# Relu, squares and low part of two blocks as one operation each, and three weight steps at later places

## The chip, the cores and the metric

The program runs on one core of a Trainium2 chip. The metric is the device time of one execution in microseconds (us). An engine works through its own queue in order: TensorE (PE, with its weight loads as PEld), VectorE (DVE), ScalarE (ACT), GpSimd (POOL) and the DMA queues (SP). A wait of one engine for another is a semaphore.

## The reference, cut to what matters

Chunked attention, then a dense MLP with a squared relu, then a top-1 mixture of eight experts, all in float32:

```python
x = attention(q, k, v, mem_k, mem_v)          # 3072 tokens, 512 wide; chunks of 32, context 16 left, 8 right
h = x @ w_in                                  # 512 -> 2048
r = np.maximum(h, 0.0)
y = (r * r) @ w_out                           # 2048 -> 512
# top-1 of 8 experts (512 -> 1024 -> 512), scaled by two gates
out[mask] = gate_w * eom * (np.maximum(y[mask] @ w1[e], 0.0) @ w2[e])
```

The change touches the dense MLP, `r * r` above all.

## The kernel before

Tokens are taken in 12 blocks of 256. A number is held as a high part that TensorE multiplies in one pass (fp32r) and a low part, the rest, also in fp32r; a product is three matmuls: high by high, high by low, low by high.

For one block `b` and one feature column group `f` of 128 (f = 0 to 15) the dense MLP is: mm1 (`ph`, 12 matmuls), relu (`r`, scaled), the square (`g`, in float32), the square again rounded to fp32r (`gh`), the low part `gl = g - gh`, and mm2 (6 matmuls into `py`, which sums over all f). In a group of two blocks most f are worked for both at once: `mm1_both` (L381) is 12 matmuls of 512 columns for the two blocks, and the two relus and mm2 follow one block at a time. For the first steps (`at[b, f] < 32`, which is blocks 0 and 1) `g` is made on ScalarE (L429), afterwards on VectorE (L431).

`seq` lists the steps: step n is one (block, f). Step n of a pair of blocks with f worked together is `mm1_both` for both, then the relu of the first block; step n + 1 is the relu of the second (L1121 to L1126). After the relu come the things planned for that step (`todo`), in the order of `turn`; at the end of a step mm2 of step n - 2 is issued. For blocks 0 and 1, f = 2 starts at step 4, and f at step 2f. The order of the queues is that of this loop: nothing is rearranged afterwards.

While blocks 0 and 1 run, the weights are converted. They arrive as 64-bit numbers in 16 tiles i0, o0, i1, o1, ..., i7, o7 of 1024 columns, two f each. One tile takes: exponent on ScalarE (`split_w_exp`, L327, "ACTIVATE ws<-raw"), a shift on VectorE (L332), two "or" steps on VectorE (L339, L343), the cast to the high part on ScalarE (`split_w_hi`, L352) and the low part on VectorE (`split_w_lo`, L357). `bits` says at which step a tile's "or" steps stand; its cast and low part stand one step later, its exponent at the end of the step of the tile before, its shift one step after that. The tile in conversion (`ws`) has two buffers, so an exponent waits for the low part of the tile two before.

Beside this runs the attention of blocks 2 and later (`plan_duo`): scores, exp, normalising, transposing the probabilities (`transpose_a`: matmuls L234, copy to `e` on ScalarE, L244), the products with v (L259).

Matmuls of the experts' pairs (`Pair`) and of its single slots come after the dense MLP; pairs use the same `gh` and `gl` pool.

Of the kernel before, what the change touches and what calls it, by code (L numbers as in the profile page):

```python
# [8 lines left out]
F32 = mybir.dt.float32  # L9
F32R = mybir.dt.float32r  # L10
# [3 lines left out]
ACTF = mybir.ActivationFunctionType  # L14
ALU = mybir.AluOpType
AX = mybir.AxisListType

P = 128
NT = 3072
D = 512  # L20
# [3 lines left out]
BLK = 256  # L24
# [22 lines left out]
WSCALE = 2.0 ** -8  # L47
# [9 lines left out]
def chunk_attention_relu2_moe_top1_kernel(ctx: ExitStack, tc, qk, vv, qt, kv, w_in, w_out, wg, wexp, consts, out):  # L57
    nc = tc.nc
# [7 lines left out]
    gp = ctx.enter_context(tc.tile_pool(name="gp", bufs=2))  # L66
# [38 lines left out]
    class Duo:  # L105
        def __init__(self, b):
            self.b = b
            self.units = (2 * b, 2 * b + 1)
            self.first, self.q, self.k, self.v = {}, {}, {}, {}
            self.ps, self.mx, self.r = {}, {}, {}  # L110
            self.e = self.at = self.x = None
            self.turned = b * TPB >= EARLY
# [209 lines left out]
    def split_w_exp(kind, g, halves=None):  # L322
        t = raw[kind, g]
        if (kind, g) not in converted:
            converted[kind, g] = tp.tile([P, 1024], F32, tag="ws", name=f"ws_{kind}{g}", bufs=2)
        for s in slices(halves):
            nc.scalar.activation(converted[kind, g][:, s], t[:, s, 1].bitcast(F32), ACTF.Abs, scale=2.0 ** -111)  # L327

    def split_w_shift(kind, g, halves=None):
        for s in slices(halves):  # L330
            li = converted[kind, g][:, s].bitcast(I32)
            nc.vector.tensor_scalar(li, li, 3, None, op0=ALU.logical_shift_left)  # L332
# [14 lines left out]
    def split_w_hi(kind, g, halves=None):  # L347
        if (kind, g) not in wh:
            w = wpool.tile([P, 2, 1024], F32R, tag=f"{kind}{g}", name=f"w{kind}{g}")
            wh[kind, g], wl[kind, g] = w[:, 0], w[:, 1]  # L350
        for s in slices(halves):
            nc.scalar.copy(wh[kind, g][:, s], converted[kind, g][:, s])  # L352
# [6 lines left out]
    def slices(halves):  # L359
        return [slice(0, 1024)] if halves is None else [slice(512 * c, 512 * c + 512) for c in halves]  # L360

    def w_in_part(w, f, k):
        return w["i", f // 2].rearrange("p (g k c) -> p g k c", g=2, k=KC)[:, f % 2, k, :]
# [2 lines left out]
        return w["o", f // 2].rearrange("p (g c) -> p g c", g=2)[:, f % 2, :]  # L366


    class Block:
        def __init__(self, b):  # L370
            self.b = b
# [9 lines left out]
        def mm1_both(self, f):  # L381
            b = self.b
            two = sorted((i % 3, i) for i in (b, b + 1))
            s = slice(two[0][0], two[1][0] + 1, two[1][0] - two[0][0])
            ph = ps_h.tile([P, D], F32, tag="h", name=f"ph{b}_{f}")
            n = 0
            for k in range(KC):
                for w, x in ((wh, xhi), (wl, xhi), (wh, xlo)):
                    nc.tensor.matmul(  # L389
                        ph.rearrange("p (s c) -> p s c", s=2),  # L390
                        lhsT=w_in_part(w, f, k),
                        rhs=x[:, s, k, :],
                        start=(n == 0),
                        stop=(n == 11),
                    )
                    n += 1
            for i, (_, of) in enumerate(two):
                blocks[of].ph = ph[:, BLK * i : BLK * i + BLK]

        def mm1(self, f):  # L400
            self.mm1_products(f)
            self.relu(f)
# [10 lines left out]
                    n += 1  # L413

        def relu(self, f):
            self.relu_r(f)
            self.relu_g(f)

        def relu_r(self, f):
            self.r = gp.tile([P, BLK], F32, tag="r", name=f"r{self.b}_{f}")  # L420
            nc.scalar.activation(self.r, self.ph, ACTF.Relu, scale=WSCALE)  # L421

        def relu_g(self, f):
            b = self.b
            early = at[b, f] < 32
            r = self.r
            g = gp.tile([P, BLK], F32, tag="g", name=f"g{b}_{f}")
            if early:
                nc.scalar.activation(g, r, ACTF.Square)  # L429
            else:  # L430
                nc.vector.tensor_tensor(g, r, r, op=ALU.mult)  # L431
            gh = gp.tile([P, BLK], F32R, tag="gh", name=f"gh{b}_{f}", bufs=3)
            nc.scalar.activation(gh, r, ACTF.Square)  # L433
            gl = gp.tile([P, BLK], F32R, tag="gl", name=f"gl{b}_{f}", bufs=3)
            nc.vector.tensor_tensor(gl, g, gh.bitcast(F32), op=ALU.subtract)  # L435
            self.g[f] = gh, gl

        def mm2(self, f):
            b = self.b
# [275 lines left out]
    class Pair(Entry):  # L715
# [13 lines left out]
        def mm1(self, f):  # L729
            p = self.entry  # L730
            ph = ps_h.tile([P, D], F32, tag="h", name=f"ph{p}p{f}")[:, :BLK]
            n = 0
            for k in range(KC):
                for part, z in ((0, self.zh), (1, self.zh), (0, self.zl)):
                    nc.tensor.matmul(
                        ph,
                        lhsT=self.w[k][:, part, f * P : f * P + P],
                        rhs=z[:, k, :],
                        start=(n == 0),
                        stop=(n == 11),  # L740
                    )
                    n += 1
            gh = gp.tile([P, BLK], F32R, tag="gh", name=f"gh{p}p{f}", bufs=3)
            nc.scalar.activation(gh, ph, ACTF.Relu)
            gl = gp.tile([P, BLK], F32R, tag="gl", name=f"gl{p}p{f}", bufs=3)
            nc.vector.scalar_tensor_tensor(gl, ph, 0.0, gh.bitcast(F32), op0=ALU.max, op1=ALU.subtract)
            self.g[f] = gh, gl

# [94 lines left out]
    tiles = [(kind, g) for g in range(8) for kind in "io"]  # L843
    duos = {b: Duo(b) for b in range(NB)}
    blocks = {b: Block(b) for b in range(NB)}


    seq, both = [], set()
    for g in range(GROUPED):
        two = (2 * g, 2 * g + 1)  # L850
# [3 lines left out]
    seq += [(NB + p, f) for p in range(NP) for f in range(F2B)]  # L854
    at = {bf: n for n, bf in enumerate(seq)}
    todo, ahead = {}, {}
    turn = {split_w_hi: 0, split_w_shift: 0, split_w_lo: 1, split_w_or: 3, split_w_exp: 4}

    def plan(n, fn, *args):
        todo.setdefault(n, []).append((fn, args))  # L860

    def plan_duo(b, s, m, t, v, last=None):
        d = duos[b]
        plan(s, d.scores)
        plan(m, d.norm)
        plan(t, d.transpose_a)
        plan(v, d.av)
        if last is None:
            plan(v, d.transpose_x_copy)
        else:  # L870
            ahead[last] = d.transpose_x_copy
        if b + 1 < NB:
            plan(s + 1, duos[b + 1].load_q, 0)
            plan(s + 1, duos[b + 1].load_q, 1)
        if 2 < b < NB - 1:
            plan(v + 1, duos[b + 1].load_kv, 1)
        if b < NB - 2:
            plan(v + 2, duos[b + 2].load_kv, 0)

    def plan_gate(b, y, l, c, r):  # L880
        bl = blocks[b]
        plan(y, bl.gate_transpose)
        plan(l, bl.gate_logits)
        plan(c, bl.gate_choose)
        plan(r, bl.gate_rank)

    bits = dict(zip(range(3, 16), (2, 4, 6, 8, 10, 12, 14, 15, 17, 18, 20, 21, 26)))
    for m, n in bits.items():
        if m > 4:
            plan(bits[m - 1], split_w_exp, *tiles[m])  # L890
            plan(bits[m - 1] + 1, split_w_shift, *tiles[m])
        if m > 3:
            plan(n, split_w_or, *tiles[m])
            plan(n + 1, split_w_hi, *tiles[m])
            plan(n + 1, split_w_lo, *tiles[m])
        if m > 6:
            plan(bits[m - 3] + 1, load_w, *tiles[m])
    plan(16, duos[2].load_q, 0)
# [6 lines left out]
    plan(23, lambda: prepare())  # L905
    n = at[2, 0]
    plan_duo(2, n - 7, n - 7, n - 4, n - 3)
    plan_duo(3, n + 1, n + 2, n + 5, n + 6)
    plan_gate(0, n + 7, n + 9, n + 15, n + 18)
    plan_duo(4, n + 11, n + 13, n + 15, n + 17)  # L910
# [2 lines left out]
    for g in range(2, GROUPED - 1):  # L913
        n = at[2 * g, 0]
# [4 lines left out]
    n = at[NB - 2, 0]  # L919
    plan_gate(NB - 4, n + 3, n + 4, n + 6, n + 9)  # L920
    plan_gate(NB - 3, n + 6, n + 8, n + 10, n + 12)
    n = at[NB, 0]
# [21 lines left out]
    for p in range(NP):  # L944
        n = at[NB + p, 0]
# [24 lines left out]
    n = at[NB, 0]  # L970
# [18 lines left out]
    with tc.manual_schedule():  # L989
# [4 lines left out]
        a, b = (0,), (1,)  # L994
# [123 lines left out]
        for n, (b, f) in enumerate(seq):  # L1118
            if n < 4:
                continue  # L1120
            if n in both:  # L1121
                blocks[b].mm1_both(f)
            if n in ahead:
                ahead[n]()
            if n in both or n - 1 in both:
                blocks[b].relu(f)  # L1126
            else:
                blocks[b].mm1(f)
            for fn, args in sorted(todo.get(n, []), key=lambda h: turn.get(h[0], 2)):
                fn(*args)  # L1130
            if n > 4:
                pb, pf = seq[n - 2]
                blocks[pb].mm2(pf)
# [148 lines left out]
```

## Time and profile before

| | before |
|---|---|
| median of 3 runs | 961.41 us (961.21 to 964.74) |
| profiled execution | 961.27 us, span 959.4 us |
| TensorE busy | 944.5 us (98%) |
| VectorE, ScalarE, GpSimd busy | 600.1, 453.0, 95.1 us |
| TensorE's granted clock | 0.999 |
| DMA | 125.51 MB, mean 131 GB/s |

Busy times are sums over the span; the idle part of TensorE has to be looked up by stretch, since the stages differ. Matmuls are pipelined, and a stall shows most exactly as idle time of the weight loads. In the rows below a line of a timeline is: start, duration, engine, source line, operation, output and inputs by their names in the program, shapes, count, and in brackets the idle time before and what ended it.

### The profile page before, as it was taken

The numbers are of one execution on the slowest core, as the hardware profiler recorded it, in microseconds if no ns is written. First come the engines' busy times: TensorE is split into PE (matmuls) and PEld (weight loads), VectorE is DVE, ScalarE is ACT, GpSimd is POOL, SyncE is SP. The second block draws the span as 40 slices with busy tenths as digits, with TensorE's granted clock in tenths as the row PEclk, the third lists the DMA queues.
The fourth block names the chain that finished last, engine by engine and source line by source line (L and its number), as shares of the span: only waits on it lengthen the run. The fifth ranks groups of instructions, "written<-read, shape, count | busy, mean of one in ns | idle before, by whom it ended". The sixth has DMA issues, their size and how long they took to land. (4 is left out here: it accounts for less than half of the span.)

```text
span 959.4 us, 19441 instructions
## 1 busy us (share of the span) xinstructions
PE 944.5 (98%) x7862; PEld 791.2 (82%) x7862; DVE 600.1 (63%) x1125; ACT 453.0 (47%) x816; POOL 95.1 (10%) x93
## 2 busy tenths in 40 slices
PE   8999999999999999999999999999999999999996
PEld 5787798888888888888888888889999999888885
DVE  6999663554445444534553454658776666799995
ACT  4687533333333233322322333545444555688885
POOL 0000000000000000000000011012222211212221
PEclk9999999999999999999999999999999999999999
DMA  9466512214020212021100106360886656443631
GB/s 358 174 219 235 170 68 99 77 24 119 24 77 24 85 58 77 24 76 59 48 1 1 45 1 247 126 241 25 333 316 237 235 206 245 187 175 132 219 124 42
DMA packets 30991, 125.51 MB, mean 131 GB/s; under 512 B 8559, under 2 KB 9071, under 8 KB 21554
## 3 DMA queue, kind: packets, MB, share of 16 engines
q1 hardware_dynamic: 25650, 110.30, 32.0%
q0 software_dynamic: 5248, 13.92, 4.0%
q8 instruction: 64, 1.05, 0.5%
q14 instruction: 29, 0.24, 0.1%
HBM read 138.65 MB, written 13.61 MB: 159 GB/s over the span
## 5 line engine op out<-in xcount | busy, mean ns | idle before, releaser
L389 PE MATMUL ph<-xhi,wi 128*128 128x512 f32 x688 | 212.7, 390 | 0.3 <-DVE wi L357 0.3
L421 ACT ACTIVATE r<-ph 128x256 f32<-128x256 f32 x192 | 72.2, 376 | 233.2 <-PE ph L389 199.1
L431 DVE TENSOR_TENSOR g<-r 128x256 f32<-128x256 f32 x160 | 67.6, 423 | 183.1 <-ACT r L421 183.0
L446 PE MATMUL py<-wo,gh 128*128 128x512 f32 x384 | 156.1, 407 | 0.8 <-ACT gh L433 0.8
L389 PEld LDWEIGHTS ph<-xhi,wi 128*128 128x128 f32 x688 | 129.1, 188 | 28.4 <-DVE wi L357 1.2
L447 PE MATMUL py<-wo,gh 128*128 128x512 f32 x384 | 150.1, 391 | 0.0
L448 PE MATMUL py<-wo,gl 128*128 128x512 f32 x384 | 150.0, 391 | 0.0
L389 PE MATMUL ph<-xlo,wi 128*128 128x512 f32 x344 | 133.9, 389 | 0.0
L686 DVE TENSOR_TENSOR x<-raw,x 128x1024 fp32r<-128x1024 f32 x88 | 103.2, 1223 | 7.0 <-ACT x L685 5.4
L435 DVE TENSOR_TENSOR gl<-g,gh 128x256 fp32r<-128x256 f32 x192 | 81.6, 425 | 29.1 <-ACT gh L433 7.3
L686 DVE TENSOR_TENSOR p<-raw,p 128x1024 fp32r<-128x1024 f32 x64 | 78.2, 1222 | 22.1 <-ACT p L685 21.0
L685 ACT CAST x<-raw 128x1024 fp32r<-128x1024 f32 x88 | 87.4, 1056 | 0.0
L446 PEld LDWEIGHTS py<-wo,gh 128*128 128x128 f32 x384 | 72.1, 188 | 17.4 <-issue 2.0
L448 PEld LDWEIGHTS py<-wo,gl 128*128 128x128 f32 x384 | 72.1, 188 | 16.1 <-DVE gl L435 0.6
L433 ACT ACTIVATE gh<-r 128x256 fp32r<-128x256 f32 x192 | 80.1, 417 | 10.6 <-PE py L447 2.3
L447 PEld LDWEIGHTS py<-wo,gh 128*128 128x128 f32 x384 | 72.3, 188 | 12.4
L543 POOL DMA_INDIRECT listd<-ent,idx x24 | 24.7, 1030 | 551.6 <-DVE idx L541 339.0
L389 PEld LDWEIGHTS ph<-xlo,wi 128*128 128x128 f32 x344 | 64.6, 188 | 13.5
L685 ACT CAST p<-raw 128x1024 fp32r<-128x1024 f32 x64 | 66.6, 1041 | 0.6 <-DMA raw<-in_wexp 0.6
L835 PE MATMUL po<-x,ht 128*128 128x512 f32 x264 | 65.5, 397 | 0.7 <-DVE ht L825 0.7
L835 PEld LDWEIGHTS po<-x,ht 128*128 128x128 f32 x264 | 48.1, 188 | 10.3 <-DVE ht L825 1.1
L705 POOL DMA_INDIRECT out<-o,slots x27 | 35.2, 1304 | 210.4 <-ACT o L701 91.4
(229 smaller groups left out, 1453.1 us busy)
## 6 DMA issues: line engine op xcount, KB each, us to landing
raw<-in_wexp SPq DMA_DIRECT2D x82, 1024.0 KB
kv<-in_kv SPq DMA_DIRECT2D x19, 880.0 KB
raw_o<-in_w_out SPq DMA_DIRECT2D x8, 1024.0 KB
raw_i<-in_w_in SPq DMA_DIRECT2D x7, 1024.0 KB
ydram<-y SPq DMA_DIRECT2D x24, 256.0 KB
q<-in_qt SPq DMA_DIRECT2D x20, 256.0 KB
qk<-in_qk SPq DMA_DIRECT2D x4, 624.0 KB
v<-in_vv SPq DMA_DIRECT2D x2, 1024.0 KB
```

What stands on the lines that cost most here:

```text
L389: nc.tensor.matmul(ph.rearrange("p (s c) -> p s c", s=2), lhsT=w_in_part(w, f, k), rhs=x[:, s, k, :], start=(n == 0), stop=(n == 11),)
L421: nc.scalar.activation(self.r, self.ph, ACTF.Relu, scale=WSCALE)
L431: nc.vector.tensor_tensor(g, r, r, op=ALU.mult)
L433: nc.scalar.activation(gh, r, ACTF.Square)
L435: nc.vector.tensor_tensor(gl, g, gh.bitcast(F32), op=ALU.subtract)
L446: nc.tensor.matmul(self.y[t], lhsT=gh[:, s], rhs=w_out_part(wh, f), start=(f == 0), stop=False)
L447: nc.tensor.matmul(self.y[t], lhsT=gh[:, s], rhs=w_out_part(wl, f), start=False, stop=False)
L448: nc.tensor.matmul(self.y[t], lhsT=gl[:, s], rhs=w_out_part(wh, f), start=False, stop=(f == NF - 1))
L685: nc.scalar.copy(w[:, 0], t)
L686: nc.vector.tensor_tensor(w[:, 1], t, w[:, 0].bitcast(F32), op=ALU.subtract)
L705: nc.gpsimd.indirect_dma_start(out=out, out_offset=bass.IndirectOffsetOnAxis(ap=slots[:, c, 0:1].bitcast(U32), axis=0), in_=self.y[t], in_ ...
L835: nc.tensor.matmul(self.po, lhsT=self.ht[:, part, f, :], rhs=w[:, wp, j * D : j * D + D], start=(f == 0 and part == 0 and wp == 0), stop=( ...
```

## The change

Relu, the rounded square, the square and the low part of two blocks are one operation of 512 columns each (`middle`, `relu_both`), all issued at the first of the two steps. The square is written over `r`, which has one buffer of 512 columns; `gh` and `gl` have two of 512 in place of three of 256. Where a block is worked alone, and in the expert pairs, two f share such a buffer by halves. The exponent of tiles 11 and 13 (o5, o6) goes to the step after, ahead of the shift (`split_w_late`), and the cast and low part of tile 15 (o7) go from step 27 to steps 28 and 29.

```diff
+    def room(b, f, n):
+        if n == D or f % 2 == 0:
+            rooms["now"] = [
+                gp.tile([P, D], dt, tag=tag, name=f"{tag}{b}_{f}", bufs=bufs)
+                for tag, dt, bufs in (("r", F32, 1), ("gh", F32R, 2), ("gl", F32R, 2))
+            ]
+        start = 0 if n == D else BLK * (f % 2)
+        return [x[:, start : start + n] for x in rooms["now"]]
+
+    def middle(ph, b, f):
+        r, hi, lo = room(b, f, ph.shape[1])
+        nc.scalar.activation(r, ph, ACTF.Relu, scale=WSCALE)
+        nc.scalar.activation(hi, r, ACTF.Square)
+        if at[b, f] < 32:
+            nc.scalar.activation(r, r, ACTF.Square)
+        else:
+            nc.vector.tensor_tensor(r, r, r, op=ALU.mult)
+        nc.vector.tensor_tensor(lo, r, hi.bitcast(F32), op=ALU.subtract)
+        return hi, lo
...
-            for i, (_, of) in enumerate(two):
-                blocks[of].ph = ph[:, BLK * i : BLK * i + BLK]
+            self.both = ph, [of for _, of in two]
+
+        def relu_both(self, f):
+            ph, two = self.both
+            parts = middle(ph, self.b, f)
+            for i, of in enumerate(two):
+                blocks[of].g[f] = tuple(x[:, BLK * i : BLK * i + BLK] for x in parts)
...
         def relu(self, f):
...
+            self.g[f] = middle(self.ph, self.b, f)
...
-            gh = gp.tile([P, BLK], F32R, tag="gh", name=f"gh{p}p{f}", bufs=3)
+            _, gh, gl = room(f"p{p}_", f, BLK)
...
+    def split_w_late(kind, g):
+        split_w_exp(kind, g)
+        split_w_shift(kind, g)
...
         if m > 4:
-            plan(bits[m - 1], split_w_exp, *tiles[m])
-            plan(bits[m - 1] + 1, split_w_shift, *tiles[m])
+            if m in (11, 13):
+                plan(bits[m - 1] + 1, split_w_late, *tiles[m])
+            else:
+                plan(bits[m - 1], split_w_exp, *tiles[m])
+                plan(bits[m - 1] + 1, split_w_shift, *tiles[m])
...
-            plan(n + 1, split_w_hi, *tiles[m])
-            plan(n + 1, split_w_lo, *tiles[m])
+            if m < 15:
+                plan(n + 1, split_w_hi, *tiles[m])
+                plan(n + 1, split_w_lo, *tiles[m])
...
+    plan(n - 4, lambda: split_w_hi(*tiles[15]))
+    plan(n - 3, split_w_lo, *tiles[15])
...
-            if n in both or n - 1 in both:
-                blocks[b].relu(f)
-            else:
+            if n in both:
+                blocks[b].relu_both(f)
+            elif n - 1 not in both:
                 blocks[b].mm1(f)
```

On ScalarE from f = 2 on, before (in a name the first number is f, the last a counter; `wi` and `wo` are casts of a weight tile, `ws` exponents):

```order
L421 ACTIVATE r_2_690<-ph_2_677 128x256
L429 ACTIVATE g_2_692<-r_2_690 128x256
L433 ACTIVATE gh_2_694<-r_2_690 128x256
L327 ACTIVATE ws_o_700<-raw_o_612 128x1024
L421 ACTIVATE r_2_702<-ph_2_677 128x256
L429 ACTIVATE g_2_704<-r_2_702 128x256
L433 ACTIVATE gh_2_706<-r_2_702 128x256
L352 CAST wi_710<-ws_i_669 128x1024
L421 ACTIVATE r_3_735<-ph_3_722 128x256
```

The same place of ScalarE now:

```order
L382 ACTIVATE r_2_680<-ph_2_667 128x512
L383 ACTIVATE gh_2_681<-r_2_680 128x512
L385 ACTIVATE r_2_680<-r_2_680 128x512
L327 ACTIVATE ws_o_689<-raw_o_607 128x1024
L352 CAST wi_691<-ws_i_659 128x1024
L382 ACTIVATE r_3_716<-ph_3_703 128x512
```

Relu and squares of both halves stand together ahead of the exponent, where the second half stood behind it.

On VectorE at the same place, before:

```order
L435 TENSOR_TENSOR gl_2_696<-g_2_692,gh_2_694 128x256
L339 SCALAR_TENSOR_TENSOR ws_i_669<-raw_i_493,ws_i_669 128x1024
L343 SCALAR_TENSOR_TENSOR ws_i_669<-raw_i_493,ws_i_669 128x1024
L435 TENSOR_TENSOR gl_2_708<-g_2_704,gh_2_706 128x256
L332 TENSOR_SCALAR ws_o_700<-ws_o_700 128x1024
L357 TENSOR_TENSOR wi_710<-ws_i_669,wi_710 128x1024
```

VectorE there now:

```order
L388 TENSOR_TENSOR gl_2_682<-r_2_680,gh_2_681 128x512
L339 SCALAR_TENSOR_TENSOR ws_i_659<-raw_i_492,ws_i_659 128x1024
L343 SCALAR_TENSOR_TENSOR ws_i_659<-raw_i_492,ws_i_659 128x1024
L332 TENSOR_SCALAR ws_o_689<-ws_o_689 128x1024
L357 TENSOR_TENSOR wi_691<-ws_i_659,wi_691 128x1024
```

The low part of both halves stands ahead of the two "or" steps; the second one behind them is gone.

On ScalarE from f = 8 to f = 10, before (the exponent of o5 stands one row ahead of the first):

```order
L421 ACTIVATE r_8_996<-ph_8_983 128x256
L429 ACTIVATE g_8_998<-r_8_996 128x256
L433 ACTIVATE gh_8_1000<-r_8_996 128x256
L352 CAST wi_1004<-ws_i_951 128x1024
L421 ACTIVATE r_8_1020<-ph_8_983 128x256
L429 ACTIVATE g_8_1022<-r_8_1020 128x256
L433 ACTIVATE gh_8_1024<-r_8_1020 128x256
L327 ACTIVATE ws_i_1030<-raw_i_971 128x1024
L421 ACTIVATE r_9_1051<-ph_9_1038 128x256
```

ScalarE there now, up to the relu of f = 10:

```order
L382 ACTIVATE r_8_930<-ph_8_917 128x512
L383 ACTIVATE gh_8_931<-r_8_930 128x512
L385 ACTIVATE r_8_930<-r_8_930 128x512
L352 CAST wi_937<-ws_i_895 128x1024
L327 ACTIVATE ws_o_939<-raw_o_863 128x1024
L327 ACTIVATE ws_i_957<-raw_i_907 128x1024
L382 ACTIVATE r_9_978<-ph_9_965 128x512
L383 ACTIVATE gh_9_979<-r_9_978 128x512
L385 ACTIVATE r_9_978<-r_9_978 128x512
L352 CAST wo_985<-ws_o_939 128x1024
L352 CAST wi_999<-ws_i_957 128x1024
L327 ACTIVATE ws_o_1001<-raw_o_943 128x1024
```

Two exponents, of o5 and i6, now stand in a row between the relus of f = 8 and f = 9, and two casts and an exponent between those of f = 9 and f = 10.

## Rows read from the trace of the kernel before

**Rows 1.** Two stretches: busy us (instructions) of each engine, granted clock, DMA.

```profile
30.00:120.00 90.00, 86.72 (x634) 70.65 (x633) 76.23 (x93) 62.75 (x118) 0.00 (x0) 1.00 0.57 201
120.00:930.00 810.00, 809.93 (x6521) 686.93 (x6520) 484.09 (x979) 359.66 (x657) 88.07 (x76) 1.00 0.33 119
```

**Rows 2.** Waits of weight loads, 30 to 120 us: total, times, longest.

```profile
PEld psx L259 <- ACT e L244: 2.6, 1, 2.6
PEld py L446 <- ACT gh L433: 1.6, 2, 1.2
PEld ph L389 <- DVE wi L357: 1.2, 2, 0.8
PEld py L448 <- DVE gl L435: 0.6, 3, 0.2
```

**Rows 3.** ScalarE in order of time, around f = 2 to 4.

```profile
40.39 1.06 ACT L352 CAST wo<-ws_o 128x1024 fp32r<-128x1024 f32 x1 [1.23 <-DVE ws_o L343]
...
45.47 1.06 ACT L352 CAST wi<-ws_i 128x1024 fp32r<-128x1024 f32 x1 [0.54 <-DVE ws_i L343]
46.43 0.38 ACT L421 ACTIVATE r<-ph 128x256 f32<-128x256 f32 x1
46.84 0.42 ACT L429 ACTIVATE g<-r 128x256 f32<-128x256 f32 x1
47.17 0.40 ACT L433 ACTIVATE gh<-r 128x256 fp32r<-128x256 f32 x1
47.83 1.18 ACT L327 ACTIVATE ws_i<-raw_i 128x1024 f32<-128x1024 f32 x1 [0.26 <-DVE wi L357]
48.88 0.39 ACT L421 ACTIVATE r<-ph 128x256 f32<-128x256 f32 x1
...
50.56 1.06 ACT L352 CAST wo<-ws_o 128x1024 fp32r<-128x1024 f32 x1 [0.52 <-DVE ws_o L343]
```

**Rows 4.** VectorE in order of time, the same turn.

```profile
46.57 1.23 DVE L357 TENSOR_TENSOR wi<-ws_i,wi 128x1024 fp32r<-128x1024 f32 x1 [0.18 <-ACT wi L352]
47.71 0.42 DVE L435 TENSOR_TENSOR gl<-g,gh 128x256 fp32r<-128x256 f32 x1
48.04 1.22 DVE L339 SCALAR_TENSOR_TENSOR ws_o<-raw_o,ws_o 128x1024 int32<-128x1024 int32 x1
49.30 1.23 DVE L343 SCALAR_TENSOR_TENSOR ws_o<-raw_o,ws_o 128x1024 int32<-128x1024 int32 x1
...
50.77 0.69 DVE L332 TENSOR_SCALAR ws_i<-ws_i 128x1024 int32<-128x1024 int32 x1
```

**Rows 5.** TensorE in order of time: first matmuls of f = 4, 6 and 8.

```profile
47.48 0.39 PE L389 MATMUL ph<-xhi,wi 128*128 128x512 f32 x1
...
58.67 0.62 PE L389 MATMUL ph<-xhi,wi 128*128 128x512 f32 x2
...
69.56 0.62 PE L389 MATMUL ph<-xhi,wi 128*128 128x512 f32 x2
```

**Rows 6.** Operations of 512 columns by shape: busy us, mean ns, idle before.

```profile
L811 ACT ACTIVATE h<-qh 128x512 f32<-128x512 f32 x22 | 11.9, 595 | 2.4 <-PE qh L798 2.4
...
L211 ACT ACTIVATE e<-e 128x512 f32<-128x512 f32 x2 | 1.3, 633 | 6.5 <-DVE e L205 6.5
...
L357 DVE TENSOR_TENSOR wi<-ws_i,wi 128x512 fp32r<-128x512 f32 x2 | 1.4, 686 | 0.0
```

**Rows 7.** TensorE and ScalarE in order of time, around f = 14.

```profile
107.79 0.39 PE L389 MATMUL ph<-xlo,wi 128*128 128x512 f32 x1
...
109.56 1.05 ACT L352 CAST wo<-ws_o 128x1024 fp32r<-128x1024 f32 x1 [3.72 <-DVE ws_o L343]
...
110.05 0.40 PE L448 MATMUL py<-wo,gl 128*128 128x512 f32 x1
...
111.55 0.99 ACT L244 COPY e<-psa 128x1024 f32<-128x1024 f32 x1
...
112.60 0.25 PE L259 MATMUL psx<-e,v 64*64 64x32 f32 x2 [2.15 <-ACT e L244]
```

More of the change, by code (lines that the diff above doesn't have):

```diff
@@ L366, in w_out_part @@
         return w["o", f // 2].rearrange("p (g c) -> p g c", g=2)[:, f % 2, :]
+    rooms = {}
+    def room(b, f, n):
[16 more added lines that the diff above has]
+        return hi, lo
     class Block:
@@ L415, in relu @@
         def relu(self, f):
[L416 to L429, printed above, removed]
-            else:
[L431 to L436, printed above, removed]
+            self.g[f] = middle(self.ph, self.b, f)
         def mm2(self, f):
@@ L742, in mm1 @@
                     n += 1
-            gh = gp.tile([P, BLK], F32R, tag="gh", name=f"gh{p}p{f}", bufs=3)
+            _, gh, gl = room(f"p{p}_", f, BLK)
             nc.scalar.activation(gh, ph, ACTF.Relu)
-            gl = gp.tile([P, BLK], F32R, tag="gl", name=f"gl{p}p{f}", bufs=3)
             nc.vector.scalar_tensor_tensor(gl, ph, 0.0, gh.bitcast(F32), op0=ALU.max, op1=ALU.subtract)
@@ L856, in chunk_attention_relu2_moe_top1_kernel @@
     todo, ahead = {}, {}
-    turn = {split_w_hi: 0, split_w_shift: 0, split_w_lo: 1, split_w_or: 3, split_w_exp: 4}
+    def split_w_late(kind, g):
+        split_w_exp(kind, g)
+        split_w_shift(kind, g)
+    turn = {split_w_late: 0, split_w_hi: 0, split_w_shift: 0, split_w_lo: 1, split_w_or: 3, split_w_exp: 4}
     def plan(n, fn, *args):
@@ L1124, in chunk_attention_relu2_moe_top1_kernel @@
                 ahead[n]()
-            if n in both or n - 1 in both:
-                blocks[b].relu(f)
-            else:
+            if n in both:
+                blocks[b].relu_both(f)
+            elif n - 1 not in both:
                 blocks[b].mm1(f)
```

## The prediction

> **What bounds the kernel now.** I read the busy time by stretch first. From 120 to 930 us TensorE is busy 809.93 of 810.00 us at full clock, so nothing that ScalarE or VectorE save there can move the end. From 30 to 120 us it is busy 86.72 of 90.00 [rows 1]. This is the stretch in which the 16 weight tiles of the first MLP are converted beside the matmuls of blocks 0 and 1. Next I read the weight loads' waits of that stretch, since TensorE's real stalls show at the load that precedes a matmul: 2.6 us for the copy of the transposed probabilities, 1.6 and 0.6 us for gh and gl, 1.2 us for a converted weight [rows 2]. These 6.0 us are all that can be won. Last I read ScalarE and VectorE in order of time, where one full turn of the weight conversion can be seen [rows 3, 4]; TensorE's own pace stands beside it [rows 5].
>
> **The turn that sets the pace.** Feature column f is worked by 24 matmuls of 512 columns: 12 of mm1, 12 of mm2. f = 6 begins at 58.67 and f = 8 at 69.56, without a wait between, so one f takes 10.89 / 2 = 5.445 us and one matmul 0.227 [rows 5]. In the same time one weight tile must be converted. The queues make a ring of this: ScalarE's cast of a tile; behind it in its queue the relu and squares of the next f; behind these, by data, VectorE's gl; behind gl in VectorE's queue the two "or" steps of the next tile; and these release the next cast. Before, the ring reads: cast 45.47, low part of that tile 46.57, gl 47.71, or 48.04, or 49.30, next cast 50.56: 5.09 us, less than 5.445, so the tiles get ahead of TensorE [rows 3, 4]. On the ScalarE side the same piece is cast to relu 0.96, relu to g 0.41, g to gh 0.33, gh 0.40, thus 2.10 us to gl's inputs, and the low part on VectorE (1.10 + 1.14 = 2.24 us after the cast) ends just after it. ScalarE's part was covered, barely.
>
> **The merged operations.** The ring now holds relu, square and square of 512 columns instead of half of them. Relu of 512 columns from PSUM is 595 ns, a 512-column ScalarE operation in SBUF 633 ns, a 512-column subtraction on VectorE 686 ns [rows 6]. A dependent successor starts some 0.03 us after the end (relu 46.43 to g 46.84 with 0.38 of work), and an independent one on VectorE about 0.09 before it (gl 47.71, 0.42 of work, next 48.04) [rows 3, 4]. So the ring becomes cast to relu 0.96, relu 0.63, square 0.66, square 0.66, gl 0.60, or 1.26, or 1.26 = 6.03 us. That is 0.94 more than before and 0.585 more than TensorE needs for one f. The second half's relu and squares, which used to run while VectorE did the "or" steps, and so cost the ring nothing, have been put in front of them. The Square of 512 columns to fp32r is not in the trace: it lies between 595 ns, the relu of that width, and 0.80 us, two halves of 0.40 [rows 3, 6]; I take 633, the row that also reads and writes SBUF. At 595 the ring is 5.95, at 0.80 it is 6.37.
>
> The Trainium skill (Perfetto Trace Analysis, Optimizing Scalar/DVE Operations) says that grouping into larger operations helps where such an engine is saturated, and that breaking instructions up may let work be completed sooner where they cause bubbles on other engines. Here the trace shows the second case: TensorE's stalls are for gh, gl and weights [rows 2], and from 30 to 120 us VectorE is busy 76.23 and ScalarE 62.75 of 90 us [rows 1]. By the first half of the rule the time would be that of the second case under the rivals, by the second half it is the forecast's.
>
> **First stretch, f = 4 to 8.** Up to the cast at 40.39 little differs. From there one turn: cast of the next tile (for f = 4, 5) at 40.39 + 6.03 = 46.42 instead of 45.47; its low part starts 1.10 later and ends at 48.75 instead of 47.80 [rows 3, 4]. f = 4 starts at 47.48 [rows 5] and its second matmul reads that low part, so TensorE already waited for it before: the lag is 0.95. Two turns on, the tile for f = 6 is done at 48.75 + 12.06 = 60.81, where the second matmul was due at 58.67 + 0.23: lag 1.91. Two more, f = 8: 72.87 against 69.79: lag 3.08 us.
>
> **Second stretch, f = 8 to 12.** Here seven steps take five tiles, and the two moved first steps act. The moved exponent steps for the tiles of f = 10 to 13 (their w_out part) now stand behind the cast, so two exponent steps, or a cast and one, come between one relu and the next. An exponent step is 1.18 long, and the next starts 1.05 after it [rows 3]; the shift is 0.69 [rows 4]. Turn from relu 8 to relu 9, by queue order: relu 8 at 77.53 (five turns after 46.42, plus 0.96); the "or" steps end at 81.30; cast 81.32; moved exponent step 82.28 to 83.46; shift; low part 84.08 to 85.31, which frees the buffer for the next exponent step at 85.34; relu 9 at 86.39. That is 8.86 us. Relu 9 to 10: chain 1.95, gl 0.60, shift 0.60, low part 1.14, or and or 2.52, cast 0.96, exponent 1.05 = 8.82; relu 10 at 95.21. Relu 10 to 11: chain 1.95, gl 0.60, or and or 2.52, cast 1.09, low part and exponent 2.31 = 8.47; relu 11 at 103.68. gh is ready 1.26 after a relu's start, gl 2.64 after it, or 4.36 at f = 8, where VectorE is late.
>
> TensorE against that (12 matmuls are 2.72 us): mm2 of f = 8 waits 0.65 for gl, mm1 of f = 10 0.93 for its weight, mm2 of f = 9 0.78 for gl, mm2 of f = 10 2.45 for gh and 0.93 for gl, mm2 of f = 11 2.10 and 0.91: 8.75 us. The waits for gh and gl that this stretch had, 1.6 + 0.6 = 2.2, are inside that [rows 2]. Net 6.55.
>
> **What is won.** The copy of the transposed probabilities stood behind the last weight's cast (109.56) and half a relu, and ran at 111.55; the products that need it started at 112.60, though TensorE's last matmul before them was issued at 110.05 [rows 7]. With that cast moved behind it, the copy follows relu and squares of f = 14: mm1 ends at 107.79 + 0.39 = 108.18, chain 1.95, copy 1.0: ready at 111.2 on the old clock, where 110.28 would be free. 0.93 is left of 2.58: 1.65 us back.
>
> **Costs of nothing.** The half tiles in the single-block steps and in the expert pairs, the single r buffer, the multiply in place, and the new buffer counts fall where TensorE is full [rows 1]; there the chain is relu 0.63, then two 0.69 on VectorE, 2.0 us, and TensorE asks for it 5.4 us later. Were that cover gone, each f would lose what is above that. In the conversion stretch the single r buffer makes each relu wait for the gl before it; the cast ahead of it in ScalarE's queue has waited for a later VectorE instruction already. The order of DMA issues is the same.
>
> **Sum.** 3.08 + 6.55 - 1.65 = 8.0 us. The profiled execution took 961.27 us, 1.9 more than its span, and the median is 961.41; 961.27 + 8.0 gives 969.3.
>
> **Rivals.**
> - The ring is slower as worked out, but the first stretch absorbs it and the second goes as before with the moved steps making room: only 3.08 is paid, the 2.2 and 1.65 are won: 960.7, no change. For it: tiles from f = 10 on are planned several steps ahead of their use. Against: the lead that those steps live on is what the first stretch eats. Chance 0.10.
> - The narrower sums decide: per f, VectorE issues 0.60 of gl instead of two of 0.33, and ScalarE saves the fixed part of three instructions. Then the waits go: 961.3 - 6.0 = 955.3, faster. For it: VectorE has hardly a gap in its rows [rows 4]. Against: this holds only if the ring stays under 5.445 us, that is if the three ScalarE operations and gl take under 1.97 us instead of 2.55, which four measured widths contradict. Chance 0.06.
> - The ring, with Squares at 0.80 us: about 0.34 more in each turn, 2.7 more over eight turns: 972. Part of the forecast's range, chance 0.04 beyond 973.
>
> **How the numbers follow.** The forecast has 0.80. Its own bounds are 595 ns Squares (0.08 less per turn, 968.6) and 972; stalls partly shared between the two stretches could take some 4 us off. The range 964.5 to 973 leaves out the two cases that are not slower and the far tail. A difference of 0.5% (4.8 us) is about what a measurement tells from no change: slower beyond 966.2: 0.81; within: 0.13; faster: 0.06.
>
> **What would show it.** Right: from 40 to 95 us casts of weight tiles 6.0 us apart instead of 5.1, VectorE idle before gl for ScalarE's second square, TensorE waiting at mm1 of f = 4, 6 and 8 about 1 us each for VectorE's low part, waits of 2 us for gh near f = 10 and 11, and about 1 us for the copy at f = 14. After about 130 us all as before, some 8 us later. Wrong: casts still 5.1 to 5.4 apart, or TensorE's waits from 30 to 120 us summing to 6 us or less.

## The result: 1.0% slower, and the profile after

The changed kernel takes 973.53 us (median of 4 runs, 971.46 to 975.12) against 961.54 of the kernel before on the same chip. The ratio is 1.0102, 95% interval 1.0083 to 1.0122: 9.8 us more (8.0 to 11.7). The two medians alone lie 12.0 us apart; the kernel before spreads over 3.5 us in its four runs here, so the text goes by the ratio with its interval. The forecast was 969.3, slower, by 8.0 us, with a range of 964.5 to 973. The median lies 0.5 us above that range; the ratio applied to the 961.27 us that the forecast started from gives 971.1, inside it. The profiled execution took 975.12 us, of which 973.3 is the span; it is the slowest of the four, where the profiled execution of before is among the quickest.

The busy time by stretch first, as in [rows 1]; the columns are the same (TensorE, weight loads, VectorE, ScalarE, GpSimd, granted clock, DMA share, GB/s). The third row is the part that holds the same work as 30 to 120 us before (633 matmuls for 634), and the last two rows are two short stretches for later.

```profile
30.00:120.00 90.00, 82.39 (x479) 64.37 (x479) 73.32 (x78) 53.56 (x72) 0.00 (x0) 0.98 0.52 184
120.00:930.00 810.00, 805.49 (x6612) 682.46 (x6611) 456.64 (x825) 332.43 (x500) 85.00 (x74) 1.00 0.34 118
30.48:129.58 99.10, 90.82 (x633) 71.20 (x632) 75.98 (x81) 58.53 (x78) 0.00 (x0) 0.98 0.53 183
96.00:100.00 4.00, 2.37 (x7) 1.63 (x8) 3.97 (x5) 2.67 (x4) 0.00 (x0) 0.86 0.44 186
100.00:104.00 4.00, 4.00 (x15) 3.12 (x14) 3.49 (x4) 1.96 (x2) 0.00 (x0) 0.71 0.53 171
```

From 30 to 120 us TensorE is busy 82.39 us instead of 86.72. VectorE and ScalarE are busy less in it too, in part because the changed kernel is late and has done less by 120 us. Over the same work ScalarE is busy 58.53 us instead of 62.75, VectorE 75.98 instead of 76.23: the smaller sum did come on ScalarE, hardly on VectorE, and it won nothing. The weight loads' waits of the same stretch (total, times, longest), beside [rows 2]:

```profile
PEld ph L411 <- DVE wi L357: 5.0, 5, 1.1
PEld py L455 <- DVE gl L388: 4.2, 5, 1.1
PEld py L453 <- ACT gh L383: 3.1, 2, 2.5
PEld ph L411 <- ACT wi L352: 0.9, 3, 0.3
```

These four are 13.2 us where before had 6.0 with the copy; the copy's wait, behind 120 us now, is 1.1. ScalarE in order of time, the turn that [rows 3] show:

```profile
40.91 1.06 ACT L352 CAST wo<-ws_o 128x1024 fp32r<-128x1024 f32 x1 [1.20 <-DVE ws_o L343]
...
46.95 1.05 ACT L352 CAST wi<-ws_i 128x1024 fp32r<-128x1024 f32 x1 [2.11 <-DVE ws_i L343]
47.90 0.59 ACT L382 ACTIVATE r<-ph 128x512 f32<-128x512 f32 x1
48.52 0.63 ACT L383 ACTIVATE gh<-r 128x512 fp32r<-128x512 f32 x1
49.18 0.63 ACT L385 ACTIVATE r<-r 128x512 f32<-128x512 f32 x1
49.72 1.12 ACT L327 ACTIVATE ws_i<-raw_i 128x1024 f32<-128x1024 f32 x1
52.97 1.06 ACT L352 CAST wo<-ws_o 128x1024 fp32r<-128x1024 f32 x1 [2.12 <-DVE ws_o L343]
```

And VectorE in the same turn, beside [rows 4]:

```profile
48.03 1.23 DVE L357 TENSOR_TENSOR wi<-ws_i,wi 128x1024 fp32r<-128x1024 f32 x1 [0.52 <-ACT wi L352]
49.85 0.69 DVE L388 TENSOR_TENSOR gl<-r,gh 128x512 fp32r<-128x512 f32 x1 [0.59 <-ACT r L385]
50.46 1.22 DVE L339 SCALAR_TENSOR_TENSOR ws_o<-raw_o,ws_o 128x1024 int32<-128x1024 int32 x1
51.71 1.22 DVE L343 SCALAR_TENSOR_TENSOR ws_o<-raw_o,ws_o 128x1024 int32<-128x1024 int32 x1
```

Cast to cast is 52.97 - 46.95 = 6.02 us; six such turns, from 40.91 to 77.07, make 36.16. Follow the ring through both lists: cast 46.95, relu 47.90, square, square, then VectorE, which has been idle 0.59 for the second square, does gl at 49.85, the two "or" steps, and only then can ScalarE, idle 2.12, cast again. Both engines have idle time in every turn, and neither could use it. What TensorE pays is seen at the load that waits:

```profile
49.31 0.19 PEld L411 LDWEIGHTS ph<-xhi,wi 128*128 128x128 f32 x1 [1.07 <-DVE wi L357]
...
73.42 0.19 PEld L411 LDWEIGHTS ph<-xhi,wi 128*128 128x128 f32 x1 [1.07 <-DVE wi L357]
...
96.98 0.19 PEld L453 LDWEIGHTS py<-wo,gh 128*128 128x128 f32 x1 [2.52 <-ACT gh L383]
```

One wait of 1.07 at f = 4, 6 and 8 (and 0.25 to 0.35 a matmul earlier for the cast), and the long one at f = 10.

### The profile page after: what moved, and what is told of

Its sections match the earlier page's. It is cut to its first block, busy times and chain, and to the rows that moved or that the text cites. A ratio compares the mean times of both kernels' runs of the same rounds, so it can differ in the third digit from the quotient of the medians.

```text
span 973.3 us, 18903 instructions
## 1 busy us (share of the span) xinstructions
PE 949.8 (98%) x7862; PEld 792.0 (81%) x7862; DVE 582.1 (60%) x967; ACT 429.1 (44%) x630; POOL 94.6 (10%) x93
## 5 line engine op out<-in xcount | busy, mean ns | idle before, releaser
L387 DVE TENSOR_TENSOR r<-r 128x512 f32<-128x512 f32 (+1 forms) x88 | 56.6, 644 | 222.7 <-ACT gh L383 222.7
L382 ACT ACTIVATE r<-ph 128x512 f32<-128x512 f32 (+1 forms) x106 | 59.0, 556 | 244.9 <-PE ph L411 211.7
L388 DVE TENSOR_TENSOR gl<-r,gh 128x512 fp32r<-128x512 f32 (+1 forms) x106 | 68.0, 642 | 20.1 <-ACT r L385 11.4
L383 ACT ACTIVATE gh<-r 128x512 fp32r<-128x512 f32 (+1 forms) x106 | 62.7, 592 | 3.4
```

Of the source, the lines that this page charges most:

```text
L382: nc.scalar.activation(r, ph, ACTF.Relu, scale=WSCALE)
L383: nc.scalar.activation(hi, r, ACTF.Square)
L387: nc.vector.tensor_tensor(r, r, r, op=ALU.mult)
L388: nc.vector.tensor_tensor(lo, r, hi.bitcast(F32), op=ALU.subtract)
```

## The experiments

Each ratio is to the kernel before on the same chip, with its 95% interval; 0.001 is 0.96 us.

**The low part behind the "or" steps.** All operations stay 512 columns wide; only gl's place on VectorE changes.

```
-        nc.vector.tensor_tensor(lo, r, hi.bitcast(F32), op=ALU.subtract)
+        if 4 <= at[b, f] < 32:
+            held.append((lo, r, hi))     # issued behind the step's weight steps
+        else:
+            nc.vector.tensor_tensor(lo, r, hi.bitcast(F32), op=ALU.subtract)
```

> The changed kernel, all of 512 columns, with one thing reordered on VectorE: in the steps 4 to 31 the low part (gl) is issued behind the weight steps that the same step plans, so behind the two "or" steps and no longer in front of them. The same instructions with the same widths. Ring theory: the ring loses ScalarE's relu and two squares and the low part (0.63 + 0.66 + 0.66 + 0.60 = 2.55 us of the 6.03), so casts follow at VectorE's and TensorE's pace, 5.5 us or less, TensorE no longer waits for weights at mm1 of f = 4, 6 and 8; the second stretch still waits for gl, which is now later by the "or" steps: 963 to 968. Rival (wide operations or the single r buffer cost by themselves, whatever their order): 971 to 975, casts 6.0 us apart.

Measured: 1.0055 (1.0036 to 1.0074), so some 4.5 us of the 9.8 come back by order alone. ScalarE's casts:

```profile
41.09 1.06 ACT L352 CAST wo<-ws_o 128x1024 fp32r<-128x1024 f32 x1 [1.22 <-DVE ws_o L343]
...
45.84 1.05 ACT L352 CAST wi<-ws_i 128x1024 fp32r<-128x1024 f32 x1 [0.83 <-DVE ws_i L343]
...
50.58 1.06 ACT L352 CAST wo<-ws_o 128x1024 fp32r<-128x1024 f32 x1 [0.80 <-DVE ws_o L343]
```

They are 4.75 and 4.74 apart, with the same widths on both engines. TensorE's waits for weights fall from 5.9 us to 0.7, and its waits for gl, which now stands behind 2.5 us of "or", rise from 4.2 to 8.2. The ring is gone; a part of its price moved to the low part.

**Halves again, in three doses.** The first kernel does relu, squares and low part per block (256 columns) while blocks 0 and 1 run beside the weight conversion; the second also puts the moved weight steps back; the third has no merged operation anywhere, only the change's buffers.

```
+            i = two.index(of)
+            r, hi, lo = (x[:, BLK * i : BLK * i + BLK] for x in self.wide)
+            nc.scalar.activation(r, ph[:, BLK * i : BLK * i + BLK], ACTF.Relu, scale=WSCALE)
...
-            if n in both:
+            if n < 32 and (n in both or n - 1 in both):
+                blocks[0].relu_one(f, b)
+            elif n in both:
```

> The changed kernel with relu, squares and low part of steps below 32 done per block again, 256 columns each, while the three moved first steps of weights stay moved. Ring theory: casts 5.1 to 5.45 us apart until 75 us and no loss there; the moved exponent steps lengthen single turns behind relu, so that 2 to 4 us are lost between 75 and 110 us and 1.5 won at the copy: 962.5 to 966. Rival (the merge and the shared buffers cost by themselves): 970 to 975. Second rival (the moves are worth what they win at the copy, nothing is lost): 960 to 961.

> The changed kernel with two parts undone: while blocks 0 and 1 run beside the weight conversion (steps below 32), relu, squares and low part are done per block again, 256 columns each, on halves of the shared buffers; and the three first steps of weights stand where they stood before. What is left of the change is the merge in the later steps, the half tiles, the single r buffer and the multiply in place. Ring theory: the turn of ScalarE and VectorE in this stretch is again cast, relu, square, square, low part of 256 columns, two "or" steps, about 5.1 us, under the 5.445 that TensorE needs, so the time is that of before plus 0 to 2 us: 961 to 963.5, casts 5.1 to 5.45 us apart. Rival A (the merge itself or the shared buffers cost wherever they stand): 966 to 974, and the waits of TensorE after 130 us grow. Rival B (the sums of instruction times decide): 963 or less and no more than before.

> The changed kernel with no merge left: relu, squares and low part of every pair of blocks are done per block, 256 columns each, in the late steps too, and the three moved weight steps stand where they stood before. What is left of the change are the buffers alone: one r instead of two and no separate g, and gh and gl as halves of two wide buffers instead of three of 256 columns. Beside the kernel with the early halves and the late merge (ratio 1.0049): if the late merge costs those 4.7 us, this one is at 1.000 to 1.002 (961.4 to 963.3); if the single r and the shared halves cost it in the conversion stretch (the copy for f = 14 waited 3.7 us instead of 2.6, gl 1.5 instead of 0.6), it stays at 1.003 to 1.006 (964.3 to 967.2).

Measured: 1.0063 (1.0043 to 1.0083), 1.0049 (1.0031 to 1.0067) and 1.0033 (1.0018 to 1.0048). The first two are 1 to 3 us above what the ring theory gave them, and the third says why: with nothing merged, what is left of the change (one r, halves of wide buffers, the square written over r) costs 3.2 us here (1.7 to 4.6). The casts are some 5.1 us apart in all three, so it is not the ring. In the kernel with the early halves and the moved steps the largest place is f = 14; ScalarE first, and then VectorE:

```profile
115.14 0.38 ACT L433 ACTIVATE r<-ph 128x256 f32<-128x256 f32 x1 [3.83 <-DVE gl L436]
...
116.32 0.99 ACT L244 COPY e<-psa 128x1024 f32<-128x1024 f32 x1
```

```profile
112.23 1.22 DVE L339 SCALAR_TENSOR_TENSOR ws_o<-raw_o,ws_o 128x1024 int32<-128x1024 int32 x1
113.48 1.23 DVE L343 SCALAR_TENSOR_TENSOR ws_o<-raw_o,ws_o 128x1024 int32<-128x1024 int32 x1
114.62 0.42 DVE L436 TENSOR_TENSOR gl<-r,gh 128x256 fp32r<-128x256 f32 x1
```

There is one r. The relu of f = 14 may not write it before the gl of the last half has read it, and that gl stands behind both "or" steps; the copy of the transposed probabilities is behind that relu in ScalarE's queue, and TensorE waits 3.2 us for it instead of 2.6. In the other two it waits 3.7 us, and there the place is f = 12, before the probabilities are made. In the third kernel, ScalarE's first relu of f = 12, and VectorE:

```profile
99.78 0.38 ACT L433 ACTIVATE r<-ph 128x256 f32<-128x256 f32 x1 [0.55 <-DVE gl L439]
...
102.26 0.43 DVE L439 TENSOR_TENSOR gl<-r,gh 128x256 fp32r<-128x256 f32 x1 [0.75 <-ACT r L436]
102.61 1.22 DVE L190 TENSOR_REDUCE mx<-pss 128x16 f32<-128x1024 f32 x1
```

The relu waits for gl, gl for the squares behind that relu, and the first operation of the probabilities (mx) stands behind both gl. Before, it starts at 99.98; the cast ahead of it comes at 96.99 here and 95.45 before, so 1.1 of its 2.6 us of lag were added in between, as much as the copy's wait grew. So these kernels are no clean undoing. What the late merge costs by itself is the second against the third: their intervals overlap, and no time is shown for it.

**The moved steps.** In one kernel they stand back beside the wide operations, in one they stand alone in the kernel before.

```
-            if m in (11, 13):            # and the last weight's cast and low part
+            if m in ():                  # as before
```

> The changed kernel with the cast of the last weight and the two first steps (exponent, shift) put back where they stood; relu, squares and low part stay 512 columns wide. Ring theory: the first stretch loses the same 3 us, the second waits for weights and gl at other places but for about the same sum, and the copy of the transposed probabilities at f = 14 waits 2.6 instead of 1.1: 970 to 974, casts 6.0 us apart from 40 to 77 us. Rival (the moved steps make the loss): below 966.

> The kernel before with only the three moved weight steps (the last weight's cast and low part behind the copy of the transposed probabilities, the exponent and shift of two weights one step later); no merge, the old buffers. Ring theory: the ring of 5.09 us is untouched; the wait for the copy falls from 2.6 to 0 to 0.5 us, the longer turns at the moved exponent steps give 1 to 2.5 us back as waits for gl and gh: ratio 0.998 to 1.001, 959.5 to 962.5. Rival (the moves lengthen each turn after f = 8 as they do beside the merge, and are the larger part of the loss): ratio 1.004 or more, 965 and over.

Measured: 1.0097 (1.0070 to 1.0123) and 1.0006 (0.9994 to 1.0019), both times as the ring theory had them: the moves do not make the loss, and no change of it by them is shown. Two details were missed: beside the wide operations the copy waits 1.7 us and not 2.6, and alone the moves give back more than the 1 to 2.5 us expected. The waits of the second, 30 to 126 us:

```profile
PEld py L448 <- DVE gl L435: 3.9, 5, 2.2
...
PEld psx L259 <- ACT e L244: 0.4, 1, 0.4
```

The copy's 2.6 went down to 0.4, and the moved exponent steps gave it back as waits for gl, 3.9 instead of 0.6.

**The kernel before, profiled again.** It tells what belongs to an execution and not to an edit.

> The kernel before, unchanged, profiled a second time on another day's chip. In all five profiles of changed kernels TensorE waits once, some 688 to 704 us in, 1.6 to 3.2 us for a gl of the third expert pair, and in four of them the granted clock falls below 1.00 for some 4 to 8 us near 100 to 120 us; the one profile of before has 0.3 us and 1.00 there. If these belong to the merge, this profile shows 0.3 us and no fall again and ends within 1 us of 961.3. If they belong to the execution (the round trip of three scattered list writes ahead of the expert weights, and the clock), this profile can show 1 to 3 us of the wait or a fall of the clock, and ends at 962 to 966.

Measured: 965.39 us, one run. It waits for gl of the third expert pair, and its clock falls:

```profile
PEld ph2p L735 <- DVE gl2p L746: 1.8, 1, 1.8
```

```profile
112.00:116.00 4.00, 3.42 (x129) 3.36 (x129) 0.60 (x2) 1.53 (x4) 0.00 (x0) 0.61 0.34 141
116.00:120.00 4.00, 4.00 (x10) 3.18 (x11) 1.23 (x1) 1.01 (x1) 0.00 (x0) 0.53 0.68 215
```

Its waits of 30 to 126 us are those of [rows 2] to a tenth. So the profile of before that the forecast used was one of the quickest executions, and a fall of the clock in the changed kernel's trace cannot be booked to the change by itself. (Near 100 to 120 us the clock falls in three of the five profiles that the expectation speaks of, not in four.) The expert pair is less clear. In the six traces whose operations behind step 32 are not merged this wait is 0.3 to 1.8 us, 0.95 in the mean; in the seven with the merge there it is 1.5 to 3.2, mean 2.0. Some 1 us may go with the late merge; no run takes it apart.

**Work in the long wait.** Ten matmuls more, whose result nobody reads, before the products of f = 10.

```
+            if n == 22:
+                for _ in range(10):
+                    nc.tensor.matmul(more, lhsT=ones, rhs=..., start=True, stop=True)
```

> The changed kernel with ten more matmuls of 512 columns, whose result nobody reads, put on TensorE in front of the products of f = 10 that waited 2.5 us for gh, so that it works on through that wait. In the changed kernel's profile the granted clock was 0.86 and 0.71 in the 8 us after this wait, which is 1.7 us of TensorE's work at the full clock. If the idle wait brings the clock down: 1.00 at 96 to 104 us, no fall, and a time 0 to 1.7 us under the changed kernel's, 970 to 973 (the filler ends before gh comes; part of the later wait for gh comes back). If the clock falls regardless of that wait: again some 0.7 to 0.9 there and 972 to 975.

Measured: 1.0081 (1.0057 to 1.0105), 972.15 us. TensorE in order of time, and the stretches:

```profile
94.70 2.33 PE L1151 MATMUL more<-ones 128*128 128x512 bf16 x10
96.98 0.50 PE L453 MATMUL py<-wo,gh 128*128 128x512 f32 x1
...
105.45 0.50 PE L453 MATMUL py<-wo,gh 128*128 128x512 f32 x1 [1.75 <-ACT gh L383]
```

```profile
96.00:100.00 4.00, 3.34 (x14) 1.94 (x13) 3.97 (x5) 2.67 (x4) 0.00 (x0) 1.00 0.43 182
100.00:104.00 4.00, 3.69 (x17) 2.70 (x15) 3.48 (x4) 1.97 (x2) 0.00 (x0) 1.00 0.54 176
```

The clock does not fall. And yet the products of f = 10 and f = 11 start at 96.98 and 105.45 in both kernels, to the hundredth: what the full clock gained TensorE gave back in waiting for the next gh. The ring sets the pace, and the slower clock ran in time that would have been waited. The products behind the copy start at 122.17 and 122.18, so the 2.6 us between the two spans come later; the two ratios, 1.0081 and 1.0102, overlap in their intervals. The Trainium skill (TensorE: Matmul & The Clock Gate, Terms) puts the penalty of throttled time at that time times the share of the clock that is held back; over the two stretches of the changed kernel that is, as an estimate, 0.14 and 0.29 of 4 us, 1.7 us. The matmuls show about that much: from 98.95 us to the first matmul of f = 12 takes 3.40 us in the changed kernel and 1.86 with the filler, 1.54 less. At the products of f = 11 the trace shows 0 of it: the page's figure is lost time only where nothing later would have been waited for.

**Three versions.** The kernel before with the last cast alone moved behind the copy; that with the weights' "or" steps evenly spaced; and the changed kernel's wide operations with an even spacing, the exponents at their old places and the low part behind the "or" steps.

```
-    bits = dict(zip(range(3, 16), (2, 4, 6, 8, 10, 12, 14, 15, 17, 18, 20, 21, 26)))
+    bits = dict(zip(range(3, 16), (2, 4, 6, 8, 9, 11, 13, 15, 17, 19, 21, 23, 26)))   # second version
+    bits = dict(zip(range(3, 16), (2, 4, 6, 8, 10, 12, 14, 16, 18, 20, 22, 24, 26)))  # third version
```

> The kernel before with one part of the change alone: the cast and low part of the last weight go behind the copy of the transposed probabilities; nothing is merged, the exponent steps stay where they were. The copy no longer stands behind that cast, so of the 2.6 us wait at f = 14 under 0.5 is left; the other waits of 30 to 126 us (3.8 us) stay, none over 1.3 us. With no long wait the granted clock should stay at 1.00 in all runs (0.998 or more in the mean), as in the kernel with all three moves, where runs of before are at 0.993 to 0.999. Together 2 us of waiting and about 1 us of clock: ratio 0.995 to 0.998. Rival (the cast that is moved delays the last weight or the copy's successors by as much): 0.9995 to 1.001, as the three moves had (1.0006).

> As the one with the last cast later, and the steps at which a weight's "or" is planned are spaced evenly from f = 8 on: 8, 9, 11, 13, 15, 17, 19, 21, 23, 26 instead of 8, 10, 12, 14, 15, 17, 18, 20, 21, 26, so that no two weights follow each other in adjacent steps late on. By the ring, turns of two steps each leave room for gl and gh, and the waits of 1.6 + 0.6 us near f = 8 to 11 go; a wait of 0.6 for a weight's transfer may come near 94 us: 0.5 to 1 us less than with the last cast alone, ratio 0.994 to 0.997. Rival (the earlier weights at step 9 and 11 wait for their transfers or delay the relu there): as with the last cast alone or up to 2 us more.

> The changed kernel with its 512-column relu, squares and low part and its moved last cast kept; the two moved exponent steps stand where they were, the "or" steps come every second step (14, 16, 18, 20, 22, 24, 26), and in steps 6 to 24 the low part is issued behind them. The wide operations stay, but the ring of low part and "or" is cut and a turn has two steps. If the loss is the ring and not the width: the waits of 30 to 126 us fall from 14.9 to 4 to 6 us, no wait of 2 us is left and the clock stays at 1.00, ratio 0.996 to 1.000. Rival (512-column operations or the shared buffers cost by themselves): 1.004 or more.

Measured: 0.9975 (0.9963 to 0.9988), 0.9954 (0.9936 to 0.9971) and 0.9973 (0.9960 to 0.9985). All three are faster than both kernels, the second by 4.4 us against before (2.8 to 6.2). Its waits from 30 to 126 us:

```profile
PEld ph L389 <- DVE wi L357: 1.2, 2, 0.7
PEld psx L259 <- ACT e L244: 0.4, 1, 0.4
...
PEld py L448 <- DVE gl L435: 0.2, 1, 0.2
```

and those of the third:

```profile
PEld ph L421 <- DVE wi L357: 1.8, 2, 1.1
PEld psx L259 <- ACT e L244: 1.2, 1, 1.2
...
PEld py L465 <- DVE gl L391: 0.4, 1, 0.4
```

The third shows that width need not cost the 1.0%: relu, squares and low part of 512 columns stand in it as in the changed kernel, and it is faster than before. The loss was their place in the ring, of which the order alone gave back 4.5 us (first experiment), and the spacing of the turns. It does not show that width costs nothing: the fair neighbour is the second version, with 256 columns and the old buffers, and the third is 1.8 us behind it, with overlapping intervals. Three details were missed: the twelve runs of the first version have mean clocks of 0.994 to 0.999 and not 0.998 or more, the second is 2.0 us ahead of the first and not 0.5 to 1 (their intervals overlap), and the profile of the third has a fall of the clock.

## Why the prediction was right, step by step

- **The turn of 6.03 us.** Worked out from single rows, measured 6.02 to 6.04 in six turns. The one width that no row had, the Square to fp32r, is 0.63, the row that was chosen.
- **First stretch, 3.08 us of lag.** Relu 8 came at 78.03, forecast 77.53. The first cast of the ring was already 0.52 late (40.91 for 40.39), but that is the execution and not the edit: ScalarE's conversion step at 13.35 us, ahead of every changed instruction, comes at 13.88 here, and in the five traces with the old buffers that cast lies between 40.19 and 41.01 (in the eight with the new ones between 40.78 and 42.20). Less this offset the lag is 3.06.
- **Second stretch, 8.75 us of waits.** Relus 9, 10 and 11 at 86.87, 95.67 and 104.13 are 8.84, 8.80 and 8.46 apart, forecast 8.86, 8.82 and 8.47. The weight loads' waits are near those forecast: 0.74 (0.65), 1.00 (0.93), 0.96 (0.78), 2.52 (2.45) and 1.09 (0.93). At f = 11 the trace has 0.59 for gh instead of 2.10, since TensorE ran at the lower clock until then; with work in the wait the same spot shows 1.75 at the matmul.
- **The copy, 1.65 won.** Its wait is 1.09, forecast 0.93.
- **The mis-sized terms: what was taken off.** From f = 4 to the copy both kernels issue the same matmuls in the same order, so their starts can be compared one by one. Before first, then after: the last matmul ahead of f = 4 and the third of f = 8, with one of the stops before between f = 8 and f = 12 (the first behind the copy is in [rows 7], at 112.60); after, also the last ahead of the copy and the first behind it.

```profile
47.26 0.39 PE L448 MATMUL py<-wo,gl 128*128 128x512 f32 x1
70.01 0.39 PE L389 MATMUL ph<-xlo,wi 128*128 128x512 f32 x1
84.29 0.39 PE L448 MATMUL py<-wo,gl 128*128 128x512 f32 x1
85.47 0.50 PE L446 MATMUL py<-wo,gh 128*128 128x512 f32 x1 [0.80 <-ACT gh L433]
85.81 0.40 PE L447 MATMUL py<-wo,gh 128*128 128x512 f32 x1
...
47.74 0.39 PE L455 MATMUL py<-wo,gl 128*128 128x512 f32 x1
73.75 0.40 PE L411 MATMUL ph<-xlo,wi 128*128 128x512 f32 x1
121.12 0.39 PE L455 MATMUL py<-wo,gl 128*128 128x512 f32 x1
122.18 0.25 PE L259 MATMUL psx<-e,v 64*64 64x32 f32 x2 [0.67 <-ACT e L244]
```

  Less the 0.48 us at the first of them, the lag is 3.26 at f = 8 (forecast 3.08) and 10.59 at the last matmul ahead of the copy (121.12 against 110.05 in [rows 7]), so the second stretch cost 7.33 (forecast 6.55). The copy won 1.49 (forecast 1.65). Together 9.1 us against the 8.0 of the sum.

  The largest miss is in the second stretch, and there in the 2.2 us taken off for the waits that the kernel before had. The forecast's own waits are reckoned from starts of matmuls, but these 2.2 are idle time of weight loads, and the matmuls lost less by them. From 84.29 over 85.47 to 85.81 two steps take 1.52 us, where the pace is twice 0.227; that is 1.06 lost, for a wait of 1.2 in [rows 2]. The smaller waits of that stretch lost some 0.35 together. So about 1.4 could be taken off and not 2.2, which is 0.8 of the 1.1, and the 8.75 itself was nearly met (7.33 + 1.4).

  The 1.65 mixes the two measures in the same way: a wait of the weight load, less a gap between matmuls. A stop shows at the weight load, but what it costs is read from the starts of the matmuls on both sides.
- **Costs of nothing.** That the single r costs nothing holds for the change as it stands, where gl is one operation ahead of the "or" steps. It is a trap for whoever undoes the widths alone: 3.2 us, with the other new buffers. The sentence that a cast in front has always waited longer was true only while a cast stands there.
- **"After about 130 us all as before."** In this trace 4 us more come later: 1.3 more at the third expert pair, two stops of TensorE of 1.0 us each at 213 to 216 us that nothing in the trace releases, and 1.1 for a probability operation. The stops and the last have no like in any other trace here, so they are put down to the profiled execution; of the first, some part may be the late merge's (above). The 9.8 us of the ratio less the 9.1 of the stretch leaves 0.7, inside the interval.
- **The rivals.** That the moved steps make room and only 3.08 is paid (0.10) falls with the waits of the second stretch. That the smaller sums decide (0.06) falls with [rows 1] against the rows above: ScalarE is busy 4.2 us less over the same work, VectorE 0.25, and the kernel is slower. The 0.80 Square is excluded by 0.63.

The Trainium skill (Perfetto Trace Analysis, Optimizing Scalar/DVE Operations) gave two cases, grouping where an engine is saturated and breaking up where it makes bubbles. The trace agrees with the second for this place in the queue. The third version above is the limit of it: with the same grouped operations, taken out of the ring, the waits for gl are 0.6 us and those for weights 2.1.

## What to carry to other kernels

When two engines hand work to each other in turns, add up one turn of the ring through both queues and compare it with the consumer's pace; the busy sums of the engines did not tell it here. An operation is free in the ring only as long as it runs beside the other engine's part, and merging two halves can take the second half out of that shadow. Before shortening an operation, look whether its place in the queue, or the spacing of the turns, is what costs: here the place of one cast and one line of step numbers won 4.4 us, and no run shows a gain by the merge.

## What the runs showed that was not expected

The granted clock, whose two levels are 2.4 GHz (1.00) and 1.2, falls behind a stop of TensorE in some executions, within one stretch of 4 us or two neighbouring ones; over such a stretch it is then 0.5 to 0.95 in the mean. It was 0.86 and 0.71 behind the 2.52 us wait of the changed kernel, and 0.61 and 0.53 behind the copy's 2.6 us in the second profile of before, where the first has 1.00 behind the same wait. With the stop filled by matmuls it stayed at 1.00, and the mean of the four runs is 0.998 to 0.999; in the two kernels where the copy waits 3.7 us all sixteen runs have 0.992 to 0.997. It is no rule: the kernel with the low part behind has waits of up to 2.38 us, that with the early halves one of 3.2, and neither profile has a fall. The third version and the kernel with the moved steps put back have one near 16 to 24 us, in the start (0.70 and 0.79 at 20 to 24). Of 19 runs of before on one chip, the seven with a mean of 0.999 have a median of 962.1 us, the eight with 0.996 or less 964.2: most of the spread of this kernel's times on that chip goes with the clock.
